# Seventeen more tiles transposed by DMA, earlier output weights and a longer warm-up in a two-problem attention kernel

## The chip, the cores and the metric

The kernel runs on one core of a Trainium2 chip. A core has a matrix engine (TensorE, PE in the profile, with its weight loads as PEld), three engines for elementwise work and reductions (VectorE or DVE, ScalarE or ACT, GpSimd or POOL) and a queueing engine (SyncE or SP) that here only issues DMAs. Sixteen DMA engines move data. The metric is the device time of one execution in microseconds (us), lower is better. A profile belongs to one execution; its span runs from the first to the last instruction.

## The reference

Two independent attention blocks, A and B, of the same shape. Their outputs stand side by side in the last dimension. All tensors are bf16.

```python
q = (x @ wq).reshape(B, Sq, Hq, Dh).transpose(0, 2, 1, 3)   # B=16, Sq=80, D=576, Hq=32, Dh=128
k = jnp.repeat(k_cache, 2, axis=1)                          # 16 key heads, Sk=512
v = jnp.repeat(v_cache, 2, axis=1)
scores = jnp.einsum("bhqd,bhkd->bhqk", q, k) * Dh ** -0.5
p = _softmax(scores, axis=-1)
o = jnp.einsum("bhqk,bhkd->bhqd", p, v)
out = o.transpose(0, 2, 1, 3).reshape(B, Sq, Hq * Dh) @ wo  # (16, 80, 576) for A, the same for B
return jnp.concatenate([a, b], axis=-1)
```

## The kernel before, in words

**Tiles.** The work is cut into 128 units U: one batch and four key heads of one problem, units 0 to 63 for A, 64 to 127 for B. Two query heads share a key head, so each key head has 160 query rows. A unit's 4 × 160 rows make five score tiles of 128 rows by 512 keys: tiles k = 1 to 4 hold the first 128 rows of one key head each, and tile k = 0, the *remainder tile*, holds the last 32 rows of all four.

**Steps of a unit.** TensorE computes the scores (line 690 for the remainder tiles, two units together after the first ones, and 704 for the others). VectorE takes the negative row maximum (713). ScalarE writes the exponential to `p_sb` with the row sum (717). VectorE inverts the row sums (723), GpSimd multiplies the tile by them (726). Then the tile is transposed: TensorE multiplies four 128 × 128 blocks with an identity into PSUM (732) and VectorE or ScalarE copies them to `pT` (739 for remainder tiles, where the planner may choose either of the two engines; 741 for the others, on VectorE). TensorE multiplies `pT` with V (779, four groups of four a unit; each reads a quarter of the remainder tile too), and ScalarE moves the result to `oT` (795).

**Remainder tiles by DMA.** For the units that `RSEL` selects, the remainder tile goes another way: SP issues a DMA transposition from `p_sb` to `pT` (745), and lines 732 and 739 are not run for it. An entry `(a, b, m)` selects the units from a to b − 1 whose number modulo 4 is in m. For a selected unit the row sums are inverted in two goes, the remainder tile's alone and the other four together (`RG`), otherwise in one. Before the change 74 units are selected. `pT` has three buffers.

**Projections and weights.** Every eight units TensorE projects the next queries (580) from `xT` and `wq_sb`; the results are scaled into `qT` (591, 592). Every 32 units it multiplies `oT` with `wo_sb` (832); sums go to `acc` (844) or `osb` (860), and SP stores `osb` (866). SP also loads K with a transposing DMA (654, five buffers), wq (551, 554) and wo (619), and transposes x of B by DMA (518). V is loaded from ScalarE's queue (658). The wo weights of each 32 units come in two halves of four pieces; `WOR` gives for each half the unit, counted from the first of the 32, whose products release the first piece, and the distance of the pieces in units.

**The start.** x of A is loaded in parts of two and three blocks (483), and each block of 128 rows is transposed on TensorE (498, five matmuls) and copied to `xT` (502). Ahead of that, TensorE multiplies constants seven times, 512 columns each (455); nothing reads the result. A small memset on VectorE (459) follows, which marks these products as done.

**Order.** All operations are added with a key, reads and writes. A planner (`_Sched.arrange`) walks through time with assumed durations per operation and per DMA, lets each engine take the waiting operation with the smallest key, and gives out PSUM banks as they become free. What comes out is a fixed order per engine, with semaphore waits between engines. An engine runs its list strictly in that order, so an operation that waits holds up all that follow it on its engine; on SP a waiting DMA holds the loads behind it. A change of `RSEL` therefore moves the neighbours of the changed operations too.

Of the kernel before, what the change touches and what calls it, by code (L numbers as in the profile page):

```python
# [13 lines left out]
LA = 13  # L14
# [18 lines left out]
QS0 = 12.0  # L33
NOC = 2
NOSB = 4
NWARM = 7
QP1 = (0.4, 1.1)
FIRST = ("x00", "w00", "x01", "w01", "k0", "w10", "k1", "v0", "k2", "k3", "v1", "w11", "k4")
LATER = dict(x10=-0.40, x11=-0.39, v2=-0.38, v3=-0.37)
# [27 lines left out]
WOC = 1.05  # L67
XDMA = True
RG = (((0, 1, 2, 3, 4),), ((0,), (1, 2, 3, 4)))
RSEL = ((18, 24, (1, 3)), (24, 45, (0, 1, 2, 3)), (47, 48, (3,)), (61, 64, (1, 3)), (64, 65, (0,)), (65, 76, (0, 1, 2, 3)), (76, 80, (1, 3)), (83, 84, (3,)), (86, 94, (1, 3)), (94, 119, (0, 1, 2, 3)), (119, 126, (0, 2)))  # L70
RDC = 0.72
RDK = 2.0
RDO = 10.0
# [11 lines left out]
LP0 = 19.0  # L85
LPS = 1.15
LPC = 29.0
WOR = (((4.0, 1.5), (12.0, 1.5)), ((8.0, 1.7), (16.0, 1.7)), ((8.0, 1.7), (16.0, 1.7)), ((9.0, 1.7), (16.5, 1.5)))
WQR = (2.0,3.5,9.5)
XR = (-12.0,1.6)  # L90

# [276 lines left out]
def bass_concat_heads__gqa_block_cached__gqa_block_cached__near_ridge_kernel(  # L368
# [10 lines left out]
    _, G, SK, DH = A_k_cache.shape  # L379
# [16 lines left out]
    with ExitStack() as es:  # L396
# [17 lines left out]
        ps = es.enter_context(nc.psum_tensor("ps", [128, 8, 512], F32))  # L414
        psb = ps[:].bitcast(BF16)
        warm = wo_sb[:, 0, 0:512]
        ones = wo_sb[:, 1, 0:128]
# [10 lines left out]
        S = _Sched()  # L428

        def R(res, ver):  # L430
            return (res, ver)
# [15 lines left out]
        def em_warmset(e):  # L447
            return e.memset(warm, 0.0)

        vw = S.bank("M")  # L450

        def em_warm(e, vw=vw):
            last = None
            for _ in range(NWARM):
                last = e.matmul(ps[:, vw.phys, :], lhsT=ones, rhs=warm, start=True, stop=True)
            return last

        def em_warmend(e):
            return e.memset(warm[:, 0:2], 0.0)

        S.add("dve", -1000, em_warmset, writes=[R(("warm",), 0)], name="warmset", stream="warmset", dur=0.25)
        S.add("pe", -990, em_warm, reads=[R(("ones",), 0), R(("warm",), 0)], writes=[R(vw, 0)],
              name="warm", stream="W", dur=NWARM * 0.427, alloc=[vw])
        S.add("dve", -980, em_warmend, reads=[R(vw, 0)], writes=[R(("warm",), 1)], name="warmend", stream="warmset")
        IDENT = R(("ident",), 0)

        def unit(g):
# [6 lines left out]
        lead[1] = QL2  # L474
        xs = acc[:].bitcast(BF16)
        XP = ((0, 2), (2, 5))
        XA = -LA - 14.0
        for half in range(NPP):
            x_ap = probs[0][0]
            for part, (k0, k1) in enumerate(XP):  # L480
                def em_ldx(e, x_ap=x_ap, half=half, k0=k0, k1=k1):
# [5 lines left out]
                      writes=[R(("xs", half * NRT + k_), 0) for k_ in range(k0, k1)], dsem="d_x%d%d" % (half, part), land=LAND["x%d%d" % (half, part)],  # L487
                      name="ldx%d.%d" % (half, part), stream="later" if half else "first", dur=0.5, cost=XC * (k1 - k0))
            for blk in range(NRT):
# [11 lines left out]
                def em_xev(e, en=None, half=half, blk=blk, vb=vb):  # L501
# [4 lines left out]
                      stream="X", dur=_mm(5, 128), lat=0.2, alloc=[vb])  # L506
                S.add(("act", "dve") if half else "act" if blk in (1, 3) else "dve", x + 0.3, em_xev, reads=[R(vb, 0)], writes=[R(("xT", half, blk), 0)],
                      name="xev%d" % rb, stream="xed" if half else "xea" if rb in (1, 3) else "xev",
                      dur=dict(act=0.52, dve=0.40), lat=0.13)

        for half in range(NPP):
            x_ap = probs[1][0]
            st0 = UPR + 16 * half - lead[NG // 2 + 2 * half]
            for ck in range(5):
                def em_ldxt(e, x_ap=x_ap, half=half, ck=ck):
# [6 lines left out]
                      writes=[R(("xT", half, b_), 1) for b_ in range(NRT)] if ck == 0 else [R(("xT", half, "t", ck), 1)],  # L522
# [7 lines left out]
        for goct in range(NG):  # L530
# [6 lines left out]
            for pi, (c0, c1) in enumerate(pieces):  # L537
# [10 lines left out]
                for j, (k0, k1, n0, n1) in enumerate(parts):  # L548
                    def em_ldw(e, wq_ap=wq_ap, q=q, wsl=wsl, n0=n0, n1=n1, k0=k0, k1=k1):
                        if k0 == 4:  # L550
# [7 lines left out]
                          writes=[R(("wq", wsl, k0 // 4, p_), wv) for p_ in range(n0 // 256, n1 // 256)],  # L558
                          dsem="d_we%d_%d_%d" % (goct, pi, j) if goct < 2 else "%s_%d" % (dsem, j),
                          name="ldw%d.%d.%d.%d" % (goct, pi, k0, n0), stream="wqa" if not goct + pi + j else strm if goct < 2 or k0 == 0 else "wqb", dur=0.5,  # L560
# [5 lines left out]
            for i in range(8):  # L566
                for c in range(2):
# [27 lines left out]
                    if prob:  # L595
                        xr += [R(("xT", half, "t", ck), 1) for ck in range(1, 5)]
                    S.add("pe", x, em_qp,
                          reads=[R(("wq", wsl, w_, i // 2), wv) for w_ in range(2)] + [R(("wqz",), 0)] + xr,
                          writes=[R(vb, 0)] + [R(("qT", qpos(goct, bl), i), goct) for bl in range(b0, b0 + nb)],
                          name="qp%d.%d.%d" % (goct, i, c), stream="Q" if goct else "Q0",  # L600
                          dur=_mm(5, n1 - n0), lat=0.2, alloc=[vb])
                    S.add(("act", "dve"), x + 0.4, em_qev, reads=[R(vb, 0)],
                          writes=[R(("qT", qpos(goct, bl), i), goct) for bl in range(b0, b0 + nb)],
                          name="qev%d.%d.%d" % (goct, i, c), stream="qev" if goct else "qev0",
                          dur=QEV[n1 - n0])

        for sg in range(2 * NPAIR):
# [4 lines left out]
            for n in range(2 * NWC):  # L612
# [4 lines left out]
                def em_ldwo(e, wo_ap=wo_ap, h0=h0, hc=hc, wc=wc, c3=c3):  # L617
# [7 lines left out]
                      writes=[R(("wo", c3, wc), sg)]  # L625
# [19 lines left out]
        for U in range(NSU):  # L645
# [3 lines left out]
            _, kc_ap, vc_ap, _, _ = probs[prob]  # L649
# [21 lines left out]
            for k in range(5):  # L671
# [11 lines left out]
                if k == 0:  # L683
                    group.append((U, vb, ks, qp, goct))
                    if len(group) == gsize[U]:
                        def em_qkr(e, group=tuple(group)):
                            last = None
                            for _, vb_, ks_, qp_, _ in group:
# [8 lines left out]
                              reads=[R(("qT", g_[3], i), g_[4]) for g_ in group for i in (1, 3, 5, 7)]  # L697
                              + [R(("kT", g_[2]), g_[0]) for g_ in group],
                              writes=[R(g_[1], 0) for g_ in group], name="qkr%d" % U, stream="S",
                              dur=len(group) * (_mm(1, 512) + 0.0105), lat=0.2, alloc=[g_[1] for g_ in group], mode=1)  # L700
                        group = []
                else:
                    def em_qk(e, gl=gl, vb=vb, ks=ks, qp=qp):
# [4 lines left out]
                          reads=[R(("qT", qp, 2 * gl), goct), R(("qT", qp, 2 * gl + 1), goct),  # L708
                                 R(("kT", ks), U)],
                          writes=[R(vb, 0)], name="qk%d" % T, stream="S", dur=_mm(1, 512), lat=0.2, alloc=[vb])  # L710
# [33 lines left out]
                def em_rtr(e, psl=psl, pts=pts):  # L744
# [4 lines left out]
                      name="max%d" % T, stream="max", dur=0.60, lat=0.13)  # L749
                S.add("act", tq + 1.1, em_exp, reads=[R(vb, 0), R(("nm", si), Q)],  # L750
                      writes=[R(("P", psl), ("e", T)), R(("rs", ss, k), U)], name="exp%d" % T, stream="exp",
                      dur=0.68, lat=0.25)
                tg = Qof[(U, rg[-1])] - LA
                if k == rg[-1]:
# [3 lines left out]
                      reads=[R(("ri", ss, rg), U), R(("P", psl), ("e", T))],  # L758
# [187 lines left out]
```

## Time and profile before

| | |
|---|---|
| time, median of 3 runs | 769.87 us (768.84 to 770.27) |
| the profiled execution | 770.14 us, of which the span is 768.4 us |
| TensorE busy | 762.2 us, 7953 matmuls |
| VectorE, ScalarE, GpSimd busy | 677.3, 610.2, 434.1 us |
| DMA | 170.24 MB, mean 222 GB/s |
| pT by DMA | 74 transpositions, median 4.9 us from issue to landing |
| K by DMA | 128 transposing loads of 512 rows × 4 × 128 |

A row of a group of instructions gives its line, engine, operation, what it writes and reads, the shapes and the count; then the busy time in us and the mean length of one in ns; then the idle time of the engine just before them and what ended it. Matmuls overlap in the pipeline, so the length of one is more than the time it takes from the next. A row of a timeline gives start and length in us, engine, line, operation and count, with the idle time ahead in brackets. A row of the windows gives, for a stretch, the busy time and the instruction count of PE, PEld, DVE, ACT and POOL, the granted TensorE clock, the busy share of the DMA engines (packets that overlap count twice, so it can pass 1) and GB/s. A DMA issue is shown as SPq or ACTq; its length is the time in which the queue issues it, not the transfer's.

### The profile page before, as it was taken

Reading aid. Unit: us, or ns where it says so; the run is one execution under the profiler, and the core shown is the slowest. Engines: PE = TensorE matmul, PEld = TensorE weight load, DVE = VectorE, ACT = ScalarE, POOL = GpSimd, SP = SyncE. Lnnn points to the kernel's source line nnn. Section 1 sums busy time; section 2 is a strip of 40 time slices with the busy share of each in tenths; the row PEclk is TensorE's granted clock in tenths of the full one; section 3 lists DMA queues with packets and bytes.
Section 4 is the critical chain, followed back from the end, with each engine's and each line's share of the span. In section 5 each row is a group of like instructions: output and inputs, shape, how many; then the busy total and the mean of one; then the engine's idle time right before and its main releaser. Section 6 shows DMA issues by size and latency. Waiting matters only on the chain.

```text
span 768.4 us, 21160 instructions
## 1 busy us (share of the span) xinstructions
PE 762.2 (99%) x7953; PEld 578.5 (75%) x7953; DVE 677.3 (88%) x1588; ACT 610.2 (79%) x1705; POOL 434.1 (56%) x647
## 2 busy tenths in 40 slices
PE   8999999999999999999999999999999999999998
PEld 5577777777777777777777777777777777777786
DVE  4999998998888898999999899888988988898982
ACT  2879988888888888787887878987888888887850
POOL 1646655756565565565646655655655645765650
DMA  8999999999999999999999999999899999999931
GB/s 226 252 243 233 234 217 275 222 207 248 200 225 210 243 262 249 256 237 190 219 217 220 222 260 237 258 227 235 205 196 216 212 213 224 233 253 231 230 94 32
DMA packets 420484, 170.24 MB, mean 222 GB/s; under 512 B 317088, under 2 KB 420000, under 8 KB 420384
## 3 DMA queue, kind: packets, MB, share of 16 engines
q1 hardware_dynamic: 354832, 103.81, 74.5%
q10 hardware_dynamic: 65552, 65.09, 28.7%
q8 instruction: 64, 1.05, 0.6%
q14 instruction: 36, 0.29, 0.1%
HBM read 87.46 MB, written 2.95 MB: 118 GB/s over the span
## 4 chain that ended last, share of the span: by engine, by line
PE 97%; DVE 2%; DMA 0%; ACT 0%; issue 0%
PE ps L580 23%; PE ps L832 21%; PE ps L779 18%; PE ps L732 16%; PE ps L704 14%; PE ps L690 4%; DVE negmax L713 1%; DMA acc<-in_A_x_dram 0%; PE ps L498 0%; DVE pT L741 0%; DVE xT L502 0%; DVE qT L592 0%; ACT xT L502 0%; DVE pT L739 0%; DVE osb L860 0%
## 5 line engine op out<-in xcount | busy, mean ns | idle before, releaser
L726 POOL TENSOR_SCALAR p_sb<-p_sb,rinv 128x512 bf16<-128x512 bf16 x640 | 431.7, 695 | 310.1 <-DVE rinv L723 310.0
L717 ACT ACTIVATE p_sb<-ps,negmax 128x512 bf16<-128x512 f32 x640 | 441.9, 696 | 84.9 <-DVE negmax L713 73.4
L713 DVE TENSOR_REDUCE negmax<-ps 128x1 f32<-128x512 f32 x640 | 425.4, 680 | 15.7 <-PE ps L704 13.5
L779 PE MATMUL ps<-pT,v_sb 128*128 128x160 bf16 x2048 | 222.0, 233 | 0.0
L741 DVE COPY pT<-ps 128x512 bf16<-128x512 bf16 x512 | 206.9, 414 | 16.3 <-PE ps L732 15.0
L732 PE MATMUL ps<-ident,p_sb 128*128 128x128 bf16 x2264 | 217.9, 219 | 0.0
L580 PE MATMUL ps<-xT,wq_sb 128*128 128x320 bf16 (+2 forms) x1280 | 214.7, 301 | 1.7 <-ACT xT L502 0.8
L779 PEld LDWEIGHTS ps<-pT,v_sb 128*128 128x128 bf16 x2048 | 164.2, 98 | 44.9 <-issue 1.3
L704 PE MATMUL ps<-kT,qT 128*128 128x512 bf16 x512 | 193.4, 379 | 0.0
L732 PEld LDWEIGHTS ps<-ident,p_sb 128*128 128x128 bf16 x2264 | 161.1, 98 | 36.5 <-issue 5.5
L832 PE MATMUL ps<-wo_sb,oT 128*128 128x288 bf16 x1280 | 170.0, 286 | 0.0
L580 PEld LDWEIGHTS ps<-xT,wq_sb 128*128 128x128 bf16 x1280 | 117.6, 98 | 52.5 <-issue 2.4
L832 PEld LDWEIGHTS ps<-wo_sb,oT 128*128 128x128 bf16 x1280 | 122.2, 98 | 35.6 <-issue 3.4
L795 ACT CAST oT<-ps 128x320 bf16<-128x320 f32 x256 | 109.4, 427 | 33.9 <-PE ps L779 32.2
L717 ACT ACTIVATION_READ_ACCUMULATOR p_sb<-ps,negmax 128x1 f32 x640 | 132.6, 207 | 0.0
L592 DVE TENSOR_SCALAR qT<-ps 128x320 bf16<-128x320 f32 (+2 forms) x148 | 71.7, 486 | 15.4 <-PE ps L580 13.2
L591 ACT ACTIVATE qT<-ps 128x320 bf16<-128x320 f32 x108 | 47.5, 440 | 13.1 <-PE ps L580 12.8
L704 PEld LDWEIGHTS ps<-kT,qT 128*128 128x128 bf16 x512 | 50.0, 98 | 2.7 <-issue 0.2
L860 DVE TENSOR_TENSOR osb<-ps,acc 128x288 bf16<-128x288 f32 x40 | 18.2, 456 | 26.4 <-PE ps L832 26.3
L723 DVE RECIPROCAL rinv<-rowsum 128x1 f32<-128x1 f32 (+2 forms) x202 | 33.7, 167 | 7.6 <-ACT p_sb L717 7.5
L690 PE MATMUL ps<-kT,qT 128*32 128x512 bf16 x512 | 39.6, 384 | 0.0
L844 ACT COPY acc<-ps 128x288 f32<-128x288 f32 x40 | 15.9, 399 | 4.1 <-PE ps L832 3.9
(19 smaller groups left out, 55.6 us busy)
## 6 DMA issues: line engine op xcount, KB each, us to landing
v_sb<-in_B_v_cache_dram ACTq DMA_DIRECT2D x64, 512.0 KB, 4.9
v_sb<-in_A_v_cache_dram ACTq DMA_DIRECT2D x60, 512.0 KB, 5.0
wo_sb<-in_A_wo_dram SPq DMA_DIRECT2D x16, 288.0 KB, 5.2
wo_sb<-in_B_wo_dram SPq DMA_DIRECT2D x16, 288.0 KB, 4.6
wq_sb<-in_B_wq_dram SPq DMA_DIRECT2D x16, 256.0 KB, 4.8
out_dram<-osb SPq DMA_DIRECT2D x40, 72.0 KB, 3.1
wq_sb<-in_A_wq_dram SPq DMA_DIRECT2D x4, 512.0 KB, 5.2
v_sb<-in_A_v_cache_dram SPq DMA_DIRECT2D x4, 512.0 KB, 5.6
```

The source lines that it names most:

```text
L580: last = e.matmul(ps[:, vb.phys, 0:n1 - n0], lhsT=wq_sb[:, wsl, ck, i * 128:(i + 1) * 128], rhs=xT[:, half, ck, n0:n1], start=(ck == 0), s ...
L592: return e.tensor_scalar(dst, src, SCALE, None, op0=AluOpType.mult)
L690: last = e.matmul(ps[32 * g4:32 * g4 + 32, vb_.phys, :], lhsT=qT[:, qp_, g4 * 160 + 128:g4 * 160 + 160], rhs=kT[:, ks_, :, g4 * 128:(g4 + ...
L704: return e.matmul(ps[:, vb.phys, :], lhsT=qT[:, qp, gl * 160:gl * 160 + 128], rhs=kT[:, ks, :, gl * 128:(gl + 1) * 128], start=True, stop= ...
L713: return e.tensor_reduce(negmax[:, si:si + 1], ps[:, vb.phys, :], axis=AX.X, op=AluOpType.max, negate=True)
L717: return e.activation(p_sb[:, psl, :], ps[:, vb.phys, :], AF.Exp, bias=negmax[:, si:si + 1], scale=1.0, accum_out=rowsum[:, ss, k:k + 1])
L726: return e.tensor_scalar(p_sb[:, psl, :], p_sb[:, psl, :], rinv[:, ss, k:k + 1], 1.0, op0=AluOpType.mult, op1=AluOpType.mult)
L732: last = e.transpose(psb[:, vt.phys, j * 128:(j + 1) * 128], p_sb[:, psl, j * 128:(j + 1) * 128], ident[:])
L741: return cp(pT[:, pts, :, 0:4, gl * 32:gl * 32 + 32], psb[:, vt.phys, 0:512].rearrange("p (j h c) -> p j h c", j=4, h=4))
L779: last = e.matmul(ps[:, vo.phys, off:off + 160], lhsT=v_sb[:, vs, gl, j * 128:(j + 1) * 128], rhs=pT[:, pts, j, :, gl * 32:gl * 32 + 32], ...
L795: return e.copy(dst, src)
L832: last = e.matmul(ps[:, vb.phys, 0:DC], lhsT=oT[:, hi, rb * 128:(rb + 1) * 128], rhs=wo_sb[:, hi, c3 * DC:(c3 + 1) * DC], start=(hi == 0), ...
```

## The change

Three edits.

1. `RSEL`: 18 units join those whose remainder tile is transposed by DMA (17, 20, 22, 49, 51, 53, 55, 57, 59, 60, 62, 85, 86, 90, 92, 125, 126, 127) and one leaves (120). That makes 91.
2. The warm-up products become eight, and two more are added, with a PSUM bank of their own, that stand in TensorE's order right behind the first ten x transpositions. VectorE's small memset now waits for both groups, and stands behind the first copy to `xT`.
3. `WOR`: the second half of the last 32 units' wo pieces is released from unit 16.0 on at a distance of 1.4, before from 16.5 at 1.5.

Up to unit 15 the order on every engine is otherwise the same as before. From there on the planner's order around the changed tiles differs on all engines. In the changed file the lines behind the warm-up stand seven lines lower.

```diff
-NWARM = 7
+NWARM = 8
+NWARM2 = 2
...
-RSEL = ((18, 24, (1, 3)), (24, 45, (0, 1, 2, 3)), (47, 48, (3,)), (61, 64, (1, 3)), (64, 65, (0,)), (65, 76, (0, 1, 2, 3)), (76, 80, (1, 3)), (83, 84, (3,)), (86, 94, (1, 3)), (94, 119, (0, 1, 2, 3)), (119, 126, (0, 2)))
+RSEL = ((17,24,(1,3)),(20,24,(0,2)),(24,45,(0,1,2,3)),(47,48,(3,)),(49,60,(1,3)),(60,76,(0,1,2,3)),(76,80,(1,3)),(83,86,(1,3)),(86,89,(2,3)),(89,119,(0,1,2,3)),(122,128,(0,2)),(125,128,(1,3)))
...
-WOR = (((4.0, 1.5), (12.0, 1.5)), ((8.0, 1.7), (16.0, 1.7)), ((8.0, 1.7), (16.0, 1.7)), ((9.0, 1.7), (16.5, 1.5)))
+WOR = (((4.0, 1.5), (12.0, 1.5)), ((8.0, 1.7), (16.0, 1.7)), ((8.0, 1.7), (16.0, 1.7)), ((9.0, 1.7), (16.0, 1.4)))
...
-        vw = S.bank("M")
-
-        def em_warm(e, vw=vw):
-            last = None
-            for _ in range(NWARM):
-                last = e.matmul(ps[:, vw.phys, :], lhsT=ones, rhs=warm, start=True, stop=True)
-            return last
+        XA = -LA - 14.0
+
+        def add_warm(key, n, dur, cls):
+            vw = S.bank(cls)
+
+            def em_warm(e):
+                last = None
+                for _ in range(n):
+                    last = e.matmul(ps[:, vw.phys, :], lhsT=ones, rhs=warm, start=True, stop=True)
+                return last
+
+            S.add("pe", key, em_warm, reads=[R(("ones",), 0), R(("warm",), 0)], writes=[R(vw, 0)],
+                  name="warm%g" % key, stream="W", dur=n * dur, alloc=[vw])
+            return vw
...
-        S.add("pe", -990, em_warm, reads=[R(("ones",), 0), R(("warm",), 0)], writes=[R(vw, 0)],
-              name="warm", stream="W", dur=NWARM * 0.427, alloc=[vw])
-        S.add("dve", -980, em_warmend, reads=[R(vw, 0)], writes=[R(("warm",), 1)], name="warmend", stream="warmset")
+        vws = [add_warm(-990, NWARM, 0.427, "M"), add_warm(XA + 0.6, NWARM2, 0.213, "S")]
+        S.add("dve", XA + 0.7, em_warmend, reads=[R(v_, 0) for v_ in vws], writes=[R(("warm",), 1)], name="warmend",
+              stream="warmset")
```

More of the change, by code (lines that the diff above doesn't have):

```diff
@@ L476, in bass_concat_heads__gqa_block_cached__gqa_block_cached__near_ridge_kernel @@
         XP = ((0, 2), (2, 5))
-        XA = -LA - 14.0
         for half in range(NPP):
```

## The prediction

> **What bounds the kernel now.** I read the page from the top, then the chain by line, TensorE's own waits, and the start in order of time. First the page's busy times and slices:
>
> ```profile
> PE 762.2 (99%) x7953; PEld 578.5 (75%) x7953; DVE 677.3 (88%) x1588; ACT 610.2 (79%) x1705; POOL 434.1 (56%) x647
> DMA  8999999999999999999999999999899999999931
> q1 hardware_dynamic: 354832, 103.81, 74.5%
> core 0: 768.4 us, clock 1.000
> ```
>
> TensorE and the 16 DMA engines both look full, so busy shares alone don't tell which of them decides. The chain of waits and the table of TensorE's waits do:
>
> ```profile
> by line: PE ps L580 22.7%; PE ps L832 20.6%; PE ps L779 18.2%; PE ps L732 16.5%; PE ps L704 14.0%; PE ps L690 4.4%; DVE negmax L713 1.2%; DMA acc<-in_A_x_dram 0.5%; PE ps L498 0.4%; DVE pT L741 0.4%; DVE xT L502 0.2%; DVE qT L592 0.1%; ACT
> PE ps L455 <- DVE wo_sb L448: 1.2, 1, 1.2
> PE ps L580 <- ACT xT L502: 0.8, 1, 0.8
> PE ps L580 <- DVE xT L502: 0.6, 1, 0.6
> PE ps L580 <- DVE qT L592: 0.3, 1, 0.3
> PE ps L498 <- DMA acc<-in_A_x_dram: 0.3, 1, 0.3
> PE ps L498 <- DVE xT L502: 0.2, 1, 0.2
> ```
>
> These six rows are all the matmul waits of the run, 3.4 us, and all lie in the first 45 us. The one on a DMA is the first x. So after the start TensorE's issue rate decides, and work taken off it shortens the span one for one while its operands stay in time. DMA, though busy in every slice, ends no TensorE wait there.
>
> **Part 1: seventeen tiles leave TensorE.** Decoding RSEL, units 17, 20, 22, 49, 51, 53, 55, 57, 59, 60, 62, 85, 86, 90, 92, 125, 126 and 127 go to the DMA path and unit 120 comes back: 18 − 1 = 17. Each takes four identity matmuls (L732) off TensorE and a PSUM copy (L739) off VectorE or ScalarE, and adds a DMA transposition (L745) on SP's queue and one more reciprocal, since the tile is then normalised alone.
>
> ```profile
> L732 PE MATMUL ps<-ident,p_sb 128*128 128x128 bf16 x2264 | 217.9, 219 | 0.0
> L739 DVE COPY pT<-ps 128x512 bf16<-128x512 bf16 x38 | 15.8, 415 | 2.3 <-PE ps L732 2.1
> L739 ACT COPY pT<-ps 128x512 bf16<-128x512 bf16 x16 | 9.5, 596 | 0.0
> L723 DVE RECIPROCAL rinv<-rowsum 128x4 f32<-128x4 f32 x74 | 12.6, 171 | 4.4 <-ACT p_sb L717 4.4
> L723 DVE RECIPROCAL rinv<-rowsum 128x1 f32<-128x1 f32 x74 | 11.4, 155 | 1.9 <-ACT p_sb L717 1.9
> L723 DVE RECIPROCAL rinv<-rowsum 128x5 f32<-128x5 f32 x54 | 9.7, 180 | 1.2 <-ACT p_sb L717 1.2
> ```
>
> The 219 ns of a matmul row is its pipelined length and no price. L732's 16.5% of the chain is 126.8 us over 2264 matmuls, 56 ns each, so a step of four costs 0.224 us of TensorE, and 17 cost 3.8 us. This lies on the path. Beside it, the VectorE and ScalarE copies come to about 17 × 0.45 = 7.7 us less, and 17 × (171 + 155 − 180) = 2.5 us more of reciprocals on VectorE: both hidden behind TensorE, and together a relief.
>
> What the step adds is paid in DMA time. No row gives one tile's engine time, so I take q1's mean: 74.5% of 768.4 us for 103.81 MB is 5.5 us a MB. A tile of 0.131 MB then costs 0.72 us of all engines, 12.3 us for the 17. On SP each issue holds the queue 1.2 us (rows below), 20 us in all, and K loads and output stores stand behind it there; POOL's order changes, not its count. All of this is hidden if engines and queue have room. Three stretches where the new tiles meet wo and wq loads, against one where the kernel before already transposes every unit's tile beside wo loads:
>
> ```profile
> core 0: us, PE busy (x) PEld busy (x) DVE busy (x) ACT busy (x) POOL busy (x), PEclk, DMA share, GB/s
> 296.00:352.00 56.00, 56.00 (x595) 43.04 (x594) 50.89 (x115) 43.94 (x122) 30.35 (x45) 1.00 1.04 239
> 352.00:382.00 30.00, 30.00 (x324) 22.95 (x322) 27.94 (x69) 24.83 (x72) 19.58 (x30) 1.00 1.13 220
> 505.00:527.00 22.00, 22.00 (x236) 17.12 (x229) 19.87 (x46) 18.12 (x54) 12.61 (x19) 1.00 1.05 231
> 634.00:672.00 38.00, 38.00 (x399) 29.11 (x398) 32.78 (x81) 31.78 (x92) 24.03 (x36) 1.00 1.20 228
> 714.00:750.00 36.00, 36.00 (x412) 29.63 (x410) 31.39 (x76) 25.22 (x70) 21.56 (x32) 1.00 0.65 158
> ```
>
> The share counts overlapping packets, so it can pass 1. From 634 to 672 us it is 1.20 and TensorE is busy all 38 us. Six tiles of 0.72 us lift the first row to at most 1.12 (6 × 0.72 / 56 = 0.08), three lift the second to 1.20, two the third to 1.12. None goes beyond what the fourth row bears, and 714 to 750, where units 125 to 127 lie, has room to spare. SP in that densest stretch, and the landing of such a transposition:
>
> ```profile
> 643.23 1.20 SPq L745 DMA_TRANSPOSE pT<-p_sb  x1
> 644.47 0.58 SPq L619 DMA_DIRECT2D wo_sb<-in_B_wo_dram  x1
> 645.10 3.69 SPq L654 DMA_TRANSPOSE kT<-in_B_k_cache_dram  x1
> 649.85 1.19 SPq L745 DMA_TRANSPOSE pT<-p_sb  x1
> DMA to landing us min/median/max: 2.4/4.9/7.4
> ```
>
> Against 2.4 to 7.4 us, the shortest lead among the new tiles is the last unit's:
>
> ```profile
> 741.52 3.37 POOL L726 TENSOR_SCALAR p_sb<-p_sb,rinv 128x512 bf16<-128x512 bf16 x5 [0.28 <-DVE rinv L723]
> 749.61 0.44 PE L779 MATMUL ps<-pT,v_sb 128*128 128x160 bf16 x4
> ```
>
> The first normalisation takes a fifth of 3.37 us and ends at 742.2; its first reader starts 7.4 us later. On the DMA path it no longer waits for the other four exponentials, so the lead grows. I price waits at zero, with ends of 0 and 12.3 us (all added engine time reaching TensorE), near zero because of the 634 row.
>
> The Trainium skill (DMA: Bandwidth & Descriptors, "Latency and other measured facts") gives 261 GB/s for a DMA transpose with a non-contiguous middle dimension. By that page a tile is an estimated 0.5 us of engine time and 17 are 8.5 us, so that where DMA decides, the change would cost about 4 us; no run here shows that rate.
>
> **Part 2: the warm-up.** The start as it is:
>
> ```profile
> 1.24 3.17 PE L455 MATMUL ps<-wo_sb 128*128 128x512 bf16 x7 [1.24 <-DVE wo_sb L448]
> 3.78 0.63 PE L455 MATMUL ps<-wo_sb 128*128 128x512 bf16 x1
> 4.70 1.22 PE L498 MATMUL ps<-ident,acc 128*128 128x128 bf16 x10 [0.28 <-DMA acc<-in_A_x_dram]
> 5.96 0.69 ACT L502 COPY xT<-ps 128x640 bf16<-128x640 bf16 x1 [3.29 <-PE ps L498]
> 6.70 2.85 PE L580 MATMUL ps<-xT,wq_sb 128*128 128x160 bf16 x20 [0.78 <-ACT xT L502]
> 9.34 1.21 PE L498 MATMUL ps<-ident,acc 128*128 128x128 bf16 x15
> 11.14 2.57 PE L580 MATMUL ps<-xT,wq_sb 128*128 128x160 bf16 x25 [0.58 <-DVE xT L502]
> ```
>
> Twenty projections take 9.34 − 6.70 = 2.64 us, 132 ns each; in the last row the same twenty take 2.57 together with five that are three times as wide (a merged row names its first shape alone). At equal time per column that is 35 units of 160 columns, about 70 ns each. So TensorE runs at half rate through the row at 6.70, though the granted clock over the run is 1.000, and at full rate at 11.14. The ten transpositions are as slow: 122 ns each against the 56 of L732.
>
> Seven warm-up products start (3.78 − 1.24) / 6 = 0.42 us apart, so an eighth starts at 4.20 and is through at 4.63, before the x-bound start at 4.70. The two new ones stand in the changed order directly behind the ten transpositions, in the gap up to 6.70 that waits for ScalarE's copy (5.96 + 0.69 = 6.65). At a cold 0.42 us each from about 5.8 on they end near 6.65: they fill the gap and delay nothing. If TensorE is at full rate from 6.7 on, the twenty save 20 × 62 ns = 1.2 us, and the next transpositions a little. VectorE's clearing memset now waits for them, with the projections' evictions queued behind it; those wait for TensorE's later projections anyway.
>
> How much of 1.2 us lives on is set by the next late thing, K:
>
> ```profile
> 28.42 2.45 SPq L654 DMA_TRANSPOSE kT<-in_A_k_cache_dram  x1
> kT<-in_A_k_cache_dram SPq DMA_TRANSPOSE x1, 5.5
> 34.50 0.61 PE L690 MATMUL ps<-kT,qT 128*32 128x512 bf16 x8
> ```
>
> The K tile issued at 28.42 lands at 33.9, only 0.6 us ahead of its reader. The DMA digits of the page stand at 8 or 9 from the first slice on, so I take its landing as fixed. What TensorE gains beyond 0.6 us it then spends waiting for K. Ends: 0 and −1.2; I take −0.5, near the K row.
>
> **Part 3: wo.** The last four output-weight pieces come half a unit (about 3 us) to 0.9 unit earlier and closer together: four issues of 0.58 us on SP, already there. TensorE never waits for wo in the six rows, so there is nothing to gain: zero, and at worst +0.6 us, one issue ahead of a K load that is needed.
>
> **Sum.** 768.4 − 3.8 − 0.5 = 764.1 us of span. The profiled run took 770.14, 1.7 us around its span, so 765.8; it stands 0.3 above the median of the runs, so 765.6.
>
> **Rivals.**
> - *The clock stays cold.* The warm-up does nothing, and part 1 stands: 769.87 − 3.8 = 766.1. For it: 4.7 us of products and transpositions from 1.24 on, with gaps of 0.1 and 0.8 us in them, did not lift the rate, and the ten transpositions may not count as work. Against it: the fifteen at 9.34 take 1.21 us, between 15 × 56 ns = 0.84 and 15 × 122 ns = 1.83, so the rate rose among transpositions, at the end of the first stretch without a gap of that size. The Trainium skill (TensorE: Matmul & The Clock Gate, "Part 4: PE-mode transpose") says that transposes don't count as busy for the clock gate; by that rule this rival holds, and the trace here doesn't exclude it.
> - *Some transpositions land late.* One that lands at the slow end (7.4 us) and stands behind one more on SP (1.2 us) misses a 7.4 us lead by 1.2 us; TensorE takes its products in order, so all wait. One to three such tiles give back 1.2 to 3.6 us: 766.8 to 769.2. Against it: none of the present 74 does it.
> - *DMA becomes the bound, slower.* From 285 to 382 us wo, wq, K and nine tiles meet; if engine time there is simply additive, 17 × 0.72 = 12.3 us come back: 769.87 + 12.3 − 4.3 = 777.9. It decides from 0.25 us per tile on, a third of the 0.72. Against it: the 1.20 row.
> - *No change.* Late tiles eat all 4.3 us: 769.9.
>
> **How the numbers follow.** Forecast 0.60; cold clock 0.15; some late 0.13; no change 0.05; slower 0.07. Measurement can tell about 0.2%, 1.5 us. Faster is the first three less the third's upper end, of which I count 0.02 as no change: 0.86; same 0.07; slower 0.07. The likeliest case alone spans 764.9 (all 1.2 us of the warm-up kept) to 766.2 (wo at its worst). The range goes below it to 764.3, by the 0.6 us the K row could move, and above to 768.2, through the cold clock and two late tiles.
>
> **What would show it.** L732's operation at 2196 matmuls at an unchanged 56 ns; 91 pT transpositions landing within about 5 us; TensorE's waits still only at the start; the first twenty projections in about 1.4 us; the K reader at about 34 us. Wrong would be waits on PV or score matmuls between 285 and 382 us, or a start of unchanged length with 2.6 us for the twenty.

## The result, and the profile after

| | median us | runs |
|---|---|---|
| before | 769.87 | 21 |
| after | 766.43 | 21 |

The ratio is 0.9964 with a 95% interval of 0.9948 to 0.9979: the changed kernel is faster, by 3.4 us in the medians and by 0.36%, 2.8 us, in the ratio, which is taken over the runs and is not the quotient of the medians. The forecast was 765.6 with a range of 764.3 to 768.2. The profiled execution took 766.66 us, 1.8 around a span of 764.9, against 770.14 and 768.4 before. The executions of one kernel are not spread evenly here: most lie within 3 us of its lowest, and some lie further above it (called long below); how many do is a result of its own, to which the experiments turn.

The page of the changed kernel, busy times and the busiest DMA queue (packets, MB, share of 16 engines):

```profile
PE 757.4 (99%) x7888; PEld 573.4 (75%) x7888; DVE 673.6 (88%) x1593; ACT 606.0 (79%) x1700; POOL 432.4 (57%) x647
...
q1 hardware_dynamic: 364080, 106.04, 76.5%
```

Its chain of waits, by line:

```profile
by line: PE ps L587 22.9%; PE ps L839 20.7%; PE ps L786 18.5%; PE ps L739 16.2%; PE ps L711 14.1%; PE ps L697 4.5%; PE ps L459 0.5%; DVE negmax L720 0.5%; PE ps L505 0.4%; ACT p_sb L724 0.4%; issue 0.2%; DVE qT L599 0.2%; DVE xT L509 0.2%; 
```

Lines behind the warm-up have moved down by seven: L739 is the matmul that was L732, L748 the copy that was L741. q1 moved 2.23 MB more, 17 tiles of 0.131 MB. Its time went from 74.5% of 768.4 us (572.5) to 76.5% of 764.9 (585.1): 12.6 us, 0.74 us a tile in this pair of profiles. The group of the identity matmuls:

```profile
L739 PE MATMUL ps<-ident,p_sb 128*128 128x128 bf16 x2196 | 211.4, 219 | 0.0
```

And the transpositions among the DMA issues, with their median landing:

```profile
pT<-p_sb SPq DMA_TRANSPOSE x91, 4.8
```

2196 matmuls are 68 fewer, four for each tile. They hold 16.2% of 764.9 us in the chain, 123.9 us, 56 ns each as before. Now all of TensorE's waits, in the table by what they waited for:

```profile
PE ps L459 <- DVE wo_sb L449: 1.2, 1, 1.2
PE ps L786 <- DVE pT L748: 1.2, 1, 1.2
PE ps L587 <- ACT xT L509: 0.7, 1, 0.7
PE ps L587 <- DVE xT L509: 0.6, 1, 0.6
PE ps L697 <- ACT oT L802: 0.5, 1, 0.5
PE ps L587 <- DVE qT L599: 0.3, 1, 0.3
```

The second row is new. The stretch of the changed kernel in order of time (start, us), SP's queue, VectorE and TensorE:

```profile
679.10 1.28 SPq L626 DMA_DIRECT2D wo_sb<-in_B_wo_dram  x1
...
685.27 1.27 SPq L752 DMA_TRANSPOSE pT<-p_sb  x1
...
690.87 0.41 DVE L748 COPY pT<-ps 128x512 bf16<-128x512 bf16 x1
...
691.70 0.44 PE L786 MATMUL ps<-pT,v_sb 128*128 128x160 bf16 x4 [1.21 <-DVE pT L748]
```

The landing of the transposition issued at 685.27, us from its issue:

```profile
pT<-p_sb SPq DMA_TRANSPOSE x1, 6.3
```

The wait is put down to a VectorE copy, but that copy ended at 691.28. The transposition of unit 116 landed at 685.27 + 6.3 = 691.6, and TensorE went on at 691.70: the releaser is the DMA. Unit 116's tile went by DMA before the change too, so this is not one of the new ones. (A unit's tile is found by counting the transpositions in SP's order, and its first reader by counting sixteen V products a unit.) The same tile and its first reader in the kernel before:

```profile
686.01 1.27 SPq L745 DMA_TRANSPOSE pT<-p_sb  x1
...
694.79 0.44 PE L779 MATMUL ps<-pT,v_sb 128*128 128x160 bf16 x4
```

There the lead, from issue to first reader, was 694.79 − 686.01 = 8.8 us. In the changed kernel TensorE was ready for the tile at 691.70 − 1.21 = 690.49, 4.3 us earlier than before, but SP issued it only 0.7 us earlier: the lead is down to 5.2 us, less than the 6.3 us of its landing. In the stretch that the prediction named for late tiles there is no wait (the last columns are granted clock, DMA share and GB/s; the share of 296 to 352 us was 1.04 before, that of 352 to 382 us 1.13):

```profile
296.00:352.00 56.00, 56.00 (x589) 42.13 (x586) 51.31 (x120) 43.88 (x124) 30.52 (x46) 1.00 1.13 245
352.00:382.00 30.00, 30.00 (x312) 22.91 (x309) 28.58 (x70) 24.41 (x69) 19.06 (x29) 1.00 1.10 228
```

Then the changed kernel's start in order of time, and the K tile that it leads up to:

```profile
1.24 3.60 PE L459 MATMUL ps<-wo_sb 128*128 128x512 bf16 x8 [1.24 <-DVE wo_sb L449]
4.63 0.95 PE L505 MATMUL ps<-ident,acc 128*128 128x128 bf16 x10
5.42 0.59 PE L459 MATMUL ps<-wo_sb 128*128 128x512 bf16 x2
6.76 1.54 PE L587 MATMUL ps<-xT,wq_sb 128*128 128x160 bf16 x20 [0.75 <-ACT xT L509]
8.14 1.04 PE L505 MATMUL ps<-ident,acc 128*128 128x128 bf16 x15
...
27.97 2.37 SPq L661 DMA_TRANSPOSE kT<-in_A_k_cache_dram  x1
...
33.69 0.62 PE L697 MATMUL ps<-kT,qT 128*32 128x512 bf16 x8 [0.47 <-ACT oT L802]
```

The landing of that K tile:

```profile
kT<-in_A_k_cache_dram SPq DMA_TRANSPOSE x1, 5.6
```

The twenty projections take 8.14 − 6.76 = 1.38 us instead of 2.64. K lands at 27.97 + 5.6 = 33.6 and its reader starts at 33.69 after a wait of 0.47: 0.81 us of the start's 1.26 live on, and K takes the rest.

So the pair of profiled executions adds up: 768.4 − 3.8 (68 matmuls at 56 ns) − 0.8 (start) + 1.2 (the late tile at 691.7) = 765.0, against the measured 764.9.

### The profile page after: what moved, and what is told of

Same layout as the page of the kernel before. It is cut to its first block, busy times and chain, and to the rows that moved or that the text cites. A ratio compares the mean times of both kernels' runs of the same rounds, so it can differ in the third digit from the quotient of the medians.

```text
span 764.9 us, 21036 instructions
## 1 busy us (share of the span) xinstructions
PE 757.4 (99%) x7888; PEld 573.4 (75%) x7888; DVE 673.6 (88%) x1593; ACT 606.0 (79%) x1700; POOL 432.4 (57%) x647
## 3 DMA queue, kind: packets, MB, share of 16 engines
q1 hardware_dynamic: 364080, 106.04, 76.5%
## 4 chain that ended last, share of the span: by engine, by line
PE 98%; DVE 1%; ACT 1%; issue 0%
PE ps L587 23%; PE ps L839 21%; PE ps L786 18%; PE ps L739 16%; PE ps L711 14%; PE ps L697 5%; PE ps L459 0%; DVE negmax L720 0%; PE ps L505 0%; ACT p_sb L724 0%; DVE qT L599 0%; DVE xT L509 0%; ACT qT L598 0%; ACT xT L509 0%; DVE pT L748 0%
## 5 line engine op out<-in xcount | busy, mean ns | idle before, releaser
L748 DVE COPY pT<-ps 128x512 bf16<-128x512 bf16 x512 | 207.2, 415 | 16.7 <-PE ps L739 16.0
L739 PE MATMUL ps<-ident,p_sb 128*128 128x128 bf16 x2196 | 211.4, 219 | 0.0
L739 PEld LDWEIGHTS ps<-ident,p_sb 128*128 128x128 bf16 x2196 | 156.1, 98 | 35.1 <-issue 5.5
L730 DVE RECIPROCAL rinv<-rowsum 128x4 f32<-128x4 f32 (+2 forms) x219 | 36.3, 167 | 7.6 <-ACT p_sb L724 7.6
```

What stands on the lines that cost most here:

```text
L739: last = e.transpose(psb[:, vt.phys, j * 128:(j + 1) * 128], p_sb[:, psl, j * 128:(j + 1) * 128], ident[:])
L748: return cp(pT[:, pts, :, 0:4, gl * 32:gl * 32 + 32], psb[:, vt.phys, 0:512].rearrange("p (j h c) -> p j h c", j=4, h=4))
```

## The experiments

The account leaves three questions. Does each part do what its term says? Why is unit 116 late? And is that one tile, or a sign that the DMA engines have less room than the prediction took them to have? Three theories of the late tile: **Q**, the new output-weight times put a piece (the 679.10 row) ahead of unit 116 on SP, and that order alone makes the wait; **L**, the tiles transposed densely around units 114 to 122 have too short a lead (time from issue to first reader) at that place; **S**, in some executions packets are slow for a while, anywhere where DMA is dense, and more tiles by DMA turn more of these spells into waits. A P tile is here a remainder tile that goes by DMA. The first three expectations set Q against a theory D, by which the DMA load of the added tiles makes the wait; L and S are two forms of D. Medians are of the runs given beside them, ratios are to the kernel before on the same chip.

**The changed kernel with the old output-weight times.**

```diff
-WOR = (..., ((9.0, 1.7), (16.0, 1.4)))
+WOR = (..., ((9.0, 1.7), (16.5, 1.5)))
```

> Changed kernel with the old WOR line. Theory Q (the earlier wo piece stands ahead of unit 116's transposition on SP and makes the 1.2 us wait): no product waits near 690 us, span about 763.7, time about 765.2, runs close together. Theory D (the added tiles' DMA load makes that wait): the wait of about 1.2 us stays, 766.4.

766.17 us (5 runs), ratio 0.9958 [0.9943, 0.9974], not to be told from the full change. TensorE in its profile:

```profile
722.60 0.45 PE L786 MATMUL ps<-pT,v_sb 128*128 128x160 bf16 x4 [0.97 <-DMA pT<-p_sb]
```

Unit 116 no longer waits, but unit 122 does, 1.0 us: the wait has moved, not gone. K landed late as well (its reader at 34.52), so this execution kept nothing of the start's gain: 768.4 − 3.8 + 1.0 = 765.6, measured span 765.5.

**The kernel before with the new output-weight times alone.**

```diff
-WOR = (..., ((9.0, 1.7), (16.5, 1.5)))
+WOR = (..., ((9.0, 1.7), (16.0, 1.4)))
```

> Kernel before with the new WOR line alone. Theory Q: a wait of about 1 us on the products of unit 116, near 694 us, time 770.9. Theory D: no wait, same time as before, 769.9.

769.64 us (12 runs), ratio 1.0003 [0.9986, 1.002], span 768.4, no TensorE wait after the start. Part 3 is not to be told from zero, as priced, and with the run above Q falls: the order can choose which tile is late, but it makes no wait by itself.

**The kernel before with the new tiles alone** (seventeen more by DMA, nothing else).

```diff
-RSEL = ((18, 24, (1, 3)), ..., (119, 126, (0, 2)))
+RSEL = ((17,24,(1,3)), ..., (122,128,(0,2)),(125,128,(1,3)))
```

> Kernel before with the new RSEL line alone. Theory Q: the 17 steps of four matmuls leave TensorE at 0.224 us each and nothing comes back: 769.9 - 3.8 = 766.1, span 764.6. Theory D: a late transposition near 690 us gives 1.2 us back: 767.3.

767.29 us (12 runs, from 765.16 on), ratio 0.9985 [0.9964, 1.0005]. Five of the 12 lie over 3 us above the lowest, and the profiled execution is one of them (771.1, span 769.4). TensorE and SP in it, in order of time:

```profile
715.56 0.61 PE L690 MATMUL ps<-kT,qT 128*32 128x512 bf16 x8 [1.23 <-ACT oT L795]
...
724.81 0.71 PE L779 MATMUL ps<-pT,v_sb 128*128 128x160 bf16 x4 [3.27 <-DMA pT<-p_sb]
726.17 0.74 PE L779 MATMUL ps<-pT,v_sb 128*128 128x160 bf16 x4
728.37 0.44 PE L779 MATMUL ps<-pT,v_sb 128*128 128x160 bf16 x4
...
715.59 1.20 SPq L745 DMA_TRANSPOSE pT<-p_sb  x1
```

The landing of the transposition issued at 715.59:

```profile
pT<-p_sb SPq DMA_TRANSPOSE x1, 9.2
```

Two windows of the same run (length, busy time and instructions of TensorE, its weight loads, VectorE, ScalarE and GpSimd, then granted clock, DMA share, GB/s):

```profile
712.00:724.00 12.00, 8.31 (x95) 6.26 (x92) 9.27 (x23) 8.53 (x24) 7.41 (x11) 1.00 1.26 183
724.00:736.00 12.00, 11.19 (x106) 8.90 (x107) 8.71 (x21) 6.90 (x19) 6.02 (x9) 0.86 0.69 147
```

A transposition landed 9.2 us after its issue, and TensorE stood for 3.3 us; a score product on a fresh K tile at 715.56 waited another 1.2. Behind the 3.3 us the four products take 0.71 and 0.74 us instead of 0.44. If the rate was one half there, the 0.86 of the second window means (1 − 0.86) × 12 / 0.5 = 3.4 us at that rate, which costs half of that, 1.7 us. The start was quick here with the old warm-up (twenty projections in 1.54 us, K reader at 32.82 instead of 34.50, −1.7). The sum is 768.4 − 3.8 − 1.7 + 1.2 + 3.3 + 1.7 = 769.1, measured 769.4. So the price of one slow spell is its waits and the slow clock behind it, here 6.2 us, more than all the tiles save.

**The kernel before with the new warm-up alone.**

```diff
-NWARM = 7
+NWARM = 8
+NWARM2 = 2
```

(with the new function for the products, as in the change)

> Kernel before with the new warm-up alone. If TensorE is at full rate from the first projections on: twenty projections in about 1.5 us, the reader of the K tile at about 33.7, time 769.9 - 0.8 = 769.1. If the clock stays cold (transpositions don't count as work): twenty projections in 2.6 us, time 769.9.

769.17 us (11 runs, ten of them from 768.83 to 769.35), ratio 0.9997 [0.9968, 1.0027], span 767.6. Its start and its K reader, in order of time:

```profile
6.81 1.54 PE L587 MATMUL ps<-xT,wq_sb 128*128 128x160 bf16 x20 [1.27 <-ACT xT L509]
33.85 0.62 PE L697 MATMUL ps<-kT,qT 128*32 128x512 bf16 x8 [0.55 <-ACT oT L802]
```

The rate is up and the K reader is 0.65 us earlier, but the median of 0.5 us less cannot be told from no change. The part works; it is small.

**The kernel before with eight products in place of seven, without the two behind the transpositions.**

```diff
-NWARM = 7
+NWARM = 8
```

> Kernel before with eight warm-up products and without the two behind the transpositions. If transpositions count as work for the clock: full rate by the first projections in nearly every run, runs about as close together as with the whole warm-up change (768.8 to 769.4). If only matmuls count: the runs spread over 768.4 to 770.7 as before, and a profile may show twenty projections in 2.6 us.

769.03 us (12 runs), ratio 0.9985 [0.9958, 1.0011], profiled 770.65. The projections in its order of time:

```profile
6.92 2.83 PE L580 MATMUL ps<-xT,wq_sb 128*128 128x160 bf16 x20 [1.01 <-ACT xT L502]
```

In this profile eight are not enough. Over all profiles, the row of the twenty projections is 1.54 to 1.66 us long in all seven kernels whose start has the two products too; without them it is 1.54 in two (the tiles alone, above, and the first fifteen tiles, below) and 2.83 to 2.85 in three (before, the output weights alone, and this one). The old start is thus quick in some executions and slow in others, and an eighth product alone does not settle it; the new one was quick in all seven. So a median should gain less from it than the profiled pair did.

**The same with transpositions in place of the products**: the kernel before with the new warm-up, each product of 512 columns replaced by four identity transpositions of 128.

```diff
-                    last = e.matmul(ps[:, vw.phys, :], lhsT=ones, rhs=warm, start=True, stop=True)
+                    for j in range(4):
+                        last = e.transpose(psb[:, vw.phys, j * 128:(j + 1) * 128], ones, ident[:])
```

> Kernel before with the warm-up change alone, in which every constant product of 512 columns is replaced by four identity transpositions of 128 columns. If transpositions count as work for the clock: the same start as with products, twenty projections in about 1.5 us, runs 768.8 to 769.4. If they don't: nothing lifts the rate before the projections themselves, twenty projections in 2.6 us or more in every run, the K reader later than 34.5, runs at 770 and above.

770.53 us (12 runs), ratio 1.0014 [0.9999, 1.003]. Its start, in order of time:

```profile
1.42 3.60 PE L460 MATMUL ps<-ident,wo_sb 128*128 128x128 bf16 x32 [1.42 <-POOL ident L438]
4.80 1.27 PE L506 MATMUL ps<-ident,acc 128*128 128x128 bf16 x10
5.87 0.89 PE L460 MATMUL ps<-ident,wo_sb 128*128 128x128 bf16 x8
6.95 1.56 PE L588 MATMUL ps<-xT,wq_sb 128*128 128x160 bf16 x20 [0.19 <-DVE wo_sb L468]
```

TensorE did nothing but transpositions up to 6.95 us, and the projections behind them ran at full rate, where the expectation had 2.6 us in every run if transpositions don't count: in this one profile they did count as work. The trace lists them as MATMUL; a start with no work at all ahead of the projections was not run. The time itself is no better than before; why the median is 770.5 is only partly seen (its K reader started at 34.67), and the rest stays open.

**Relief at the late place**: the changed kernel with units 114, 116, 118 and 122 back on TensorE (87 tiles by DMA).

```diff
-(89,119,(0,1,2,3)),(122,128,(0,2)),(125,128,(1,3))
+(89,113,(0,1,2,3)),(113,119,(1,3)),(124,128,(0,2)),(125,128,(1,3))
```

> Changed kernel, but units 114, 116, 118 and 122 keep their remainder tiles on TensorE (87 by DMA instead of 91). Theory L (in the stretch from 680 to 725 us transpositions and K tiles land so close to their readers that one slow DMA stalls TensorE): four steps of 0.224 us come back, 0.9, and the stalls go: no wait for a landing after 45 us, no long runs, median 766.4 or a little below, lowest run about 765.7. Theory S (stalls come with any slow DMA, wherever the tiles are): the same long runs as the changed kernel's, median about 767.3.

767.84 us (12 runs), ratio 0.9992 [0.9966, 1.0018]. The profiled execution, 767.41, has no wait after the start, but four of the 12 runs took 772.7 to 773.9. The long ones are still there with the tight place taken out, so L falls as their cause. For the waits of about 1 us near 690 to 725 us in the profiles above, L is not excluded: they are gone from this one profile.

**The first fifteen of the added tiles alone** (units 17 to 92), the rest as before (89 tiles).

```diff
-RSEL = ((18, 24, (1, 3)), ..., (119, 126, (0, 2)))
+RSEL = ((17,24,(1,3)), ..., (89,119,(0,1,2,3)),(119,126,(0,2)))
```

> Kernel before with the fifteen early units alone (17 to 92); the tail as before, with unit 120 by DMA and 125 to 127 on TensorE, old warm-up and WOR. 15 x 0.224 = 3.4 us leave TensorE. If the tail's new selection makes the stalls near 690 to 725 us: none here, 766.3 and close runs. If the fifteen early ones do, by bringing TensorE ahead of DMA: stalls as with all seventeen, 767 to 768, with runs over 770.

766.43 us (12 runs), ratio 0.9954 [0.9926, 0.9982]: 15 tiles give as much as the whole change, and the tiles of the last units add nothing that can be measured. The start was quick in its profile (span 766.0), and a score product still waits 1.2 us at 716.62, where nothing was added.

**The fifteen with the new warm-up.**

```diff
-(89,119,(0,1,2,3)),(122,128,(0,2)),(125,128,(1,3))
+(89,119,(0,1,2,3)),(119,126,(0,2))
```

(the changed kernel with this, and with the old output-weight times)

> The fifteen early units and the new warm-up, tail selection and WOR as before: 15 x 0.224 = 3.4 us and the cold start's 0.5 less: 765.8. If the tail's selection is what makes the long runs, fewer of them than in the changed kernel; otherwise as many.

765.74 us (12 runs, eight of them from 765.42 to 765.98), ratio 0.997 [0.9946, 0.9994]: the lowest median of all, but not to be told from the changed kernel. The profiled execution is a long one, 772.87. TensorE and SP in it, in order of time:

```profile
533.47 2.12 PE L839 MATMUL ps<-wo_sb,oT 128*128 128x288 bf16 x16 [2.25 <-DMA wo_sb<-in_B_wo_dram]
542.30 0.62 PE L697 MATMUL ps<-kT,qT 128*32 128x512 bf16 x8 [2.93 <-issue]
...
527.03 7.27 SPq L661 DMA_TRANSPOSE kT<-in_B_k_cache_dram  x1
```

The landings of the two pieces that TensorE waited for:

```profile
wo_sb<-in_B_wo_dram SPq DMA_DIRECT2D x1, 288.0 KB, 10.0
kT<-in_B_k_cache_dram SPq DMA_TRANSPOSE x1, 15.2
```

The window around both, with the same columns as above:

```profile
505.00:543.00 38.00, 32.82 (x341) 24.70 (x339) 29.34 (x69) 26.34 (x73) 18.79 (x29) 1.00 1.29 172
```

Here output weights and K are late, not a P tile, and over 150 us ahead of the waits in the profiles above. TensorE lost 5.2 of the 38 us. The engines moved 172 GB/s at a share of 1.29. The same window of the changed kernel has no wait in it:

```profile
505.00:543.00 38.00, 38.00 (x396) 29.13 (x394) 33.74 (x80) 30.90 (x87) 22.68 (x34) 1.00 1.18 233
```

That less was moved could be a result of TensorE's waits, since buffers come free later. It is not the whole of it: from 512 to 524 us TensorE was still busy all the time in both. First the run above, then the changed kernel:

```profile
512.00:524.00 12.00, 12.00 (x126) 9.25 (x124) 10.16 (x24) 9.06 (x27) 5.60 (x9) 1.00 1.30 176
```

```profile
512.00:524.00 12.00, 12.00 (x125) 9.22 (x123) 10.17 (x25) 9.06 (x27) 5.61 (x9) 1.00 1.13 262
```

**Five tiles moved**: the changed kernel with the old output-weight times, units 114, 116, 118 and 122 on TensorE, units 46, 78, 80, 81 and 82 by DMA instead (92 tiles).

```diff
+(46,47,(2,)),(78,79,(2,)),(80,83,(0,1,2)),
-(89,119,(0,1,2,3)),(122,128,(0,2)),(125,128,(1,3))
+(89,113,(0,1,2,3)),(113,119,(1,3)),(124,128,(0,2)),(125,128,(1,3))
```

> Changed kernel with the old WOR; the remainder tiles of units 114, 116, 118 and 122 go back to TensorE and those of 46, 78, 80, 81 and 82 go by DMA instead (92 tiles). TensorE has one step of 0.224 us less than in the changed kernel. Theory L (the stretch from 680 to 725 us is too full): fewer long runs than the changed kernel, no wait on a landing there, median about 765.5. Theory S (long runs come wherever DMA is slow in that run): about a quarter of the runs long again, median 766.5.

769.47 us (12 runs, from 765.76 on), ratio 0.9989 [0.997, 1.0008]; seven of 12 over 3 us above the lowest. Its profiled execution, 771.29, has this wait:

```profile
514.98 0.61 PE L697 MATMUL ps<-kT,qT 128*32 128x512 bf16 x8 [2.77 <-issue]
```

The landing of the K tile that it waited for:

```profile
kT<-in_B_k_cache_dram SPq DMA_TRANSPOSE x1, 13.0
```

The window behind it, at a granted clock of 0.86:

```profile
515.00:527.00 12.00, 12.00 (x106) 8.69 (x107) 8.66 (x20) 6.88 (x19) 3.77 (x6) 0.86 1.18 230
```

K again, and a stretch at half rate behind it, at a place that the five tiles don't touch. S had expected a quarter of the runs long and a median of 766.5; it is worse than that. Thinning one place and filling others gained nothing that shows.

**Every P tile of units 17 to 127 by DMA** (111 tiles, old output-weight times).

```diff
-RSEL = ((17,24,(1,3)), ..., (125,128,(1,3)))
+RSEL = ((17,128,(0,1,2,3)),)
```

> Changed kernel with every remainder tile from unit 17 on by DMA (111 tiles, 20 more than the change) and the old WOR. If TensorE still decides: 20 x 0.224 = 4.5 us less than the changed kernel, 762. If the DMA engines decide from here on: 20 x 0.72 us = 14 us of engine time come through in part, waits of TensorE on landings in many places, 768 or more.

780.44 us (12 runs, from 771.95 on), ratio 1.0098 [1.0067, 1.013]. TensorE's largest wait by cause, in a profiled execution of 775.7:

```profile
PE ps L697 <- issue: 7.8, 2, 5.4
```

The longest of them in order of time:

```profile
310.14 1.04 PE L697 MATMUL ps<-kT,qT 128*32 128x512 bf16 x8 [5.37 <-issue]
```

Here the slower rival has come true. From the changed kernel's ratio to this one are 1.34%, 10.3 us; with the 4.5 us that twenty tiles beyond the change save TensorE by count, they cost 14.8 us, 0.74 us a tile if all twenty are charged alike. By the medians (14.0 us apart, on two chips) it is 18.5 us, 0.9 a tile. Score products on fresh K tiles wait 7.8 us, 5.4 of it at 310. Somewhere between 91 and 111 tiles the late landings come to cost more than all added tiles save.

**The long executions, counted.** Runs over 3 us above the lowest of their own set (one kernel on one chip):

| kernel | long | of |
|---|---|---|
| before (all its runs) | 10 | 114 |
| 74 tiles, other parts changed (wo alone, both warm-ups, transposed warm-up) | 6 | 47 |
| 91 tiles, the changed kernel | 7 | 21 |
| 91 tiles with old wo; tiles alone | 0; 5 | 5; 12 |
| 87; 89; 89 and warm-up; 92 moved | 4; 2; 3; 7 | 12 each |
| 111 tiles | 10 | 12 |

With 74 tiles it is 16 of 161, a tenth; with 87 to 92 tiles 28 of 86, a third. The kernel before has fewer long runs in each of the four sets too: 3 of 29 beside 5 of 17 with more tiles, 5 of 35 beside 6 of 24, 1 of 29 beside 10 of 24, 1 of 21 beside 7 of 21. Place, output-weight order and warm-up make no difference that these counts could show; more tiles do. That is what S expects, but each selection also has its own order on SP, which the counts don't separate from the number.

The profiles show one part of it: the margins shrink. With 74 tiles (five profiles) the shortest lead of a P tile is 8.1 to 8.6 us, and after the start no P or K tile lands later than 1.2 us before its reader, though a K tile takes up to 14.2 us (the warm-up alone). With 87 to 92 tiles (seven profiles) the shortest lead, up to the time at which TensorE was ready, is 5.2 to 8.3 us, and in six of the seven a P tile, a K tile or both land after that time. The late P tiles are 116, 120 and 122, which all went by DMA before; the eighteen units that joined have leads of 10.4 us and more in the changed kernel and in the tiles alone. What slows the packets in some executions and not in others isn't settled by any run here.

## Why the prediction was right, and where it was off

- **TensorE's issue rate decides, and each tile is worth 0.224 us.** Right: 2196 matmuls at 56 ns, −3.8 us. The fifteen tiles alone, 15 × 0.224 = 3.4 us, measured 0.46% of 769 us, 3.5 (the interval allows 1.4 to 5.7).
- **0.72 us of DMA time a tile, 12.3 us in all.** The pair gives 0.74 and 12.6, but that it came so close is luck: with the same 74 tiles the share of q1 lies between 74.4% of 768.4 us (output weights alone) and 76.2% of 768.9 (transposed warm-up), 571.7 to 585.9 us, and with 91 tiles between 585.1 and 600.9 (78.5% of 765.5, old output weights). The means of the five and the three such profiles are 16.4 us apart, 0.96 a tile. The shares worked out from it for the three stretches, 1.12, 1.20 and 1.12, came as 1.13, 1.10 and 1.20. The Trainium skill's rate (DMA: Bandwidth & Descriptors, "Latency and other measured facts"), by which the 17 were an estimated 8.5 us, is not what this trace shows.
- **Waits priced at zero, because a DMA share of 1.20 had been borne.** This step failed. The share of a stretch says how much packet time overlaps, not how much room is left: 1.18 goes without a wait from 505 to 543 us in the changed kernel, 1.26 with 8.31 of 12 us of TensorE in the tiles alone. What the latter lacks is movement, 183 GB/s. Even that is no clean line: the changed kernel's wait at 691.7 us came in a window of 1.26 and 218 GB/s (first fence), and the kernel with units 114 to 122 relieved bore 1.25 and 211 without a wait (second fence):

```profile
675.00:693.00 18.00, 16.79 (x174) 12.68 (x172) 15.54 (x38) 13.43 (x41) 9.84 (x15) 1.00 1.26 218
```

```profile
505.00:543.00 38.00, 38.00 (x396) 29.15 (x395) 34.18 (x81) 30.51 (x85) 23.21 (x35) 1.00 1.25 211
```

- **A lead of 7.4 us against landings of 2.4 to 7.4.** This failed too. The lead was taken for the new tiles alone, in the old order: in the changed kernel's profile the eighteen have leads of 11.5 us and more, and none is late. Late is unit 116, an old tile, whose lead fell from 8.8 to 5.2 us because TensorE came 4.3 us earlier and SP's issue only 0.7. In the kernel before, unit 120 (issued at 705.54) already landed 1.2 us ahead of its reader, so the old tiles had little to give. And one execution's slowest landing was taken as the limit: in others P tiles took 9.2 us and K 13.0 and 15.2. In the profiled pair the term is +1.2 us where zero stood; in the long executions profiled it is 4.5 us and more, the half rate behind the waits included.
- **Warm-up −0.5, with K as the cap.** The mechanism was right on each step: the two products fill the gap (5.42 to 6.0), the twenty take 1.38 us (1.4 was forecast), K's reader moves to 33.69 and then waits for K. The size was 0.8 in the profiled pair and about 0.5 in the median of the warm-up alone, where the interval also holds no gain. The landing of K, taken as fixed at 33.9, came at 33.6, and at 34.4 in the run with the old output-weight times.
- **Wo at zero.** Nothing speaks against it: 1.0003 [0.9986, 1.002] alone.
- **The cold-clock rival.** It fell: the clock rose in every profile with the new products. The twenty projections behind nothing but transpositions took 1.56 us. The rule of the Trainium skill (TensorE: Matmul & The Clock Gate, "Part 4: PE-mode transpose") that transposes don't count as busy disagrees with that one profile, and the measurement decides, with the limit that the trace doesn't show whether the transpose mode of that page was on.
- **The rival of tiles that land late.** It came true beside the forecast, in part: one late tile in the profiled execution, at 691.7, not in the named stretch from 285 to 382 us, where TensorE was busy all the time. The reason the prediction gave against it, that none of the old 74 did it, was a statement about one execution and about the old leads.
- **The slower rival.** With 17 tiles it did not come, with 37 it did, and the price a tile of the last twenty (0.74 by the ratios, 0.9 by the medians) is near its 0.72 or above.
- **The sum.** −3.8 − 0.8 + 1.2 instead of −3.8 − 0.5 + 0: in the profiled pair the wait and the start's larger gain partly cancel, and it is luck that the time came within a microsecond of the forecast with the wait mispriced. The median gained 3.4 us instead of 4.3. Without the long executions the medians are 769.7 and 765.9, 3.8 apart. That fits a third of the executions paying for late DMA, and some of the old starts being quick already; no run splits the difference between the two.

## What to carry to other kernels

Price an offload from a full engine by the engine's issue time per instruction, and the engine that takes it by its own time per piece; then find how many pieces the second one bears by going past it in one run, since its busy share doesn't tell. When the full engine gets faster and the queue that feeds it does not, the leads of all transfers shrink, not just those of the new ones: list the shortest leads of the old ones too. A margin read from one profiled execution is one draw: where transfers are dense, compare the leads with the slowest landing of several executions. Judge such a change by the whole set of its times, the share of long ones too, and stop adding where the last pieces no longer move the median; here none beyond fifteen did so measurably.

## What the runs showed that was not expected

- A TensorE wait of 2.8 to 3.3 us in the middle of the run was followed by 3.4 us at half clock (in the tiles alone, the fifteen with the warm-up, and the moved tiles), about 1.7 us more on top of each such wait. Shorter waits were not: behind the changed kernel's 1.2 us the granted clock is 1.00 from 690 to 702 us, and the 2.25 us at 533.47 lies in a window of 1.00.
- In the one profile of it, identity transpositions alone brought the start to full rate, as products of 512 columns do.
- The same unchanged start is at full rate in two profiles and at half in two, 1.3 us on the first twenty projections without any edit to it (and at half in the one with an eighth product).
- In one stretch of 38 us the DMA engines moved 172 GB/s at a share of 1.29 in one execution and 233 GB/s at 1.18 in another: the share was higher where less was moved. One K tile then took 15.2 us to land, and one 13.0 in the moved tiles, against 4.1 to 11.0 over the changed kernel's profile. A slow landing alone is not the loss: in the warm-up alone one of 14.2 us made nobody wait.
